# Moving the gate's weight rows by a few bytes in on-chip memory: banded attention with a gated linear unit on one Trainium2 core

## The chip, the cores and the metric

The kernel runs on one core of one Trainium2 chip. The core has a matrix engine (PE, whose weight loads are a stream of their own, PEld), a vector engine (DVE), a scalar engine (ACT), a general engine (POOL), a queue that issues transfers (SP) and 16 transfer engines (DMA). The metric is the device time of one launch in microseconds (us), as the median of several runs. Before the change three runs gave 852.70, 850.37 and 852.55 us, a median of 852.55 us.

## The reference, cut to what matters

Eight batches, eight heads, 512 local and 32 global positions, head size 64. Local positions attend to a band of 32 positions to each side and to the 32 global ones; global positions attend to all 544. What comes out, 8 x 544 = 4352 rows of 512 numbers, goes through a gated linear unit without a nonlinearity.

```python
s_ll = scale * np.matmul(q_l, k_l.transpose(0, 1, 3, 2))
mask = np.abs(pos[:, None] - pos[None, :]) <= window          # window = 32
s_ll = np.where(mask, s_ll, -1000000000.0)
s_l = np.concatenate([scale * np.matmul(q_l, k_g.transpose(0, 1, 3, 2)), s_ll], axis=-1)
out_l = np.matmul(sm(s_l), np.concatenate([v_g, v_l], axis=2))
...
x = np.ascontiguousarray(attn_out.transpose(0, 2, 1, 3)).reshape(B * S, H * D)
a = x @ w1
b = x @ w2
h = a * b @ w3
return (h @ w_out).astype(np.float32)
```

## The kernel before, in words

The 64 heads are worked off one after another: scores, softmax over the band, the product with v. Four pairs of heads make one batch's rows of x, turned so that the 512 features lie on 4 x 128 partitions and the tokens along the row. Behind each batch two passes of the gate run over 256 tokens each, woven between the next batch's attention steps; the rows of the global positions (8 x 32 = 256 tokens) make a seventeenth pass near the end. `w3` and `w_out` are multiplied with each other at the start (L917), so that a pass has only two layers: `first` (x with w1 and w2, L771 to L782) and `second` (the gated product with w3 times w_out, L810 to L812).

Numbers are split into a high and a low part, and each product is made from three matmuls on a 4-byte type: high with high, low of x with high of w, and high of x with low of w. These are the three lines L780, L781 and L782. In `first`, the row block `m` (0 to 7) of the output features and the half `c` (0 is w1, tile `ap`; 1 is w2, tile `bp`) choose a 128 x 128 piece of the weights for each of the four pairs `k`. So one call is twelve matmuls, and a pass has 16 calls. Over 17 passes this is 3264 matmuls, each with its own weight load. x is the operand that streams through PE (256 columns of 4 bytes, so 1024 bytes a partition); the weights are the operand that is loaded (128 columns, 512 bytes a partition). The weight load for the next matmul runs while the matmul ahead of it streams its x.

The weights lie in `W12[m]`, made by `alloc_w12` (L860): before the change a high and a low tile of `[128, 4, 2, 128]` words, 4096 bytes a partition each. They are filled once near the start of the span, blocks 0 to 3 in 512-word pieces and blocks 4 to 7 in 256-word pieces, by casts (L417, high part) and subtractions (L420, low part) on ACT, DVE and POOL, and stay for the whole launch. Blocks 4 to 7 take the place of the tiles of the opening (`wo`, `raw`, `w3f`), which are given up before.

By the addresses in the built program, all pieces of the weights start at a multiple of 256 bytes. The x tiles of the sixteen ordinary passes all start 192 bytes behind such a multiple, high and low part alike. Only the pass over the global positions differs, since its x borrows other tiles (`split_x`, L752): for pair 0 the high part starts at 128 and the low part at 0, for pair 1 at 192 and 64, for pairs 2 and 3 at 192 like all others. Below, the distance is the start of the weights less the start of x, modulo 256 bytes. Before the change it is 64 everywhere but in the pass over the global positions, where it is 128, 0 and 128 in the three matmuls of pair 0, and 64, 192 and 64 in those of pair 1.

What runs when is written out by hand: `ORDER_OF` gives every step its place in one list of all steps, and the engine for those that could run on several. Each engine works off its own steps in that order, with waits on the other engines where data or buffers ask for it.

Of the kernel before, what the change touches and what calls it, by code (L numbers as in the profile page):

```python
# [8 lines left out]
F32R = mybir.dt.float32r  # L9
# [21 lines left out]
START = (("s", 0), ("sg", 0), ("s", 1), ("sg", 1), ("s", 2), ("tg", 0))  # L31

# [9 lines left out]
def i(ap):  # L42
# [36 lines left out]
    load="9 6 49 79 389 416 974 1176 1480 1586 1810 1999 2236 2405 2762 2649 3179 1 3 58 14 16 142 56 75 160 140 203 "  # L79
# [4 lines left out]
    clear="0 22 7 4 2 10 530 524 536 517",  # L84
    warm="5 25",
    fetch="8 11 12 36 46 52 72 84 100 116 126 150 171 178 200 225 246 253 272 288 309 326 349 366 377 387 426 413 "
    "447 480 471 503 174 242 147 605 617 622 638 670 682 694 730 744 737 768 791 808",
    unit="24 23 31 35 37 43 45 42 48 64 65 68 77 76 81 94 86 96 112 109 114 119 118 122 141 133 144 149 148 165 173 "
# [7 lines left out]
    fold="53 71 90 131 157 195 207 213 66 87 97 102 162 202 218 226 264 269 291 308 321 324 329 332 258 276 296 315 "  # L96
    "347 353 356 364 360 370 374 381 395 402 410 417 407 421 424 436 442 448 457 463 452 485 523 527 548 560 583 588 "
    "493 497 515 538 554 566 572 579",
    w34h="A221 D237 D339 A378 A422 A468 A594 A585",
    w34l="254 250 350 386 431 472 598 589",  # L100
    qgh="A18 A19 P231 A322 P844 P925 P1291 D1294 A1704 A1772 P2121 P2136 P2569 P2638 D3000 P3049",
    qgl="P21 P20 P265 P331 D990 D949 D1298 D1299 D1790 P1842 P2189 D2166 D2576 P2644 D3104 D3074",
    vgh="D532 P565 A546 A561 P1093 P1149 D1141 A1101 A1549 A1573 P1552 D1559 P1964 P1984 A1995 D1990 P2383 A2407 "
    "A2411 D2420 P2811 P2872 D2855 A2847 P3241 A3253 D3269 P3289",
    vgl="D537 P587 P558 P590 D1152 P1156 P1143 P1121 D1555 D1584 D1579 P1561 P2036 P2031 D2003 P2007 P2429 D2424 "
    "P2441 D2438 D2835 P2897 D2908 P2865 P3265 D3271 D3283 D3292",
    Kh="D13 A47 D99 A177 P299 A439 A668 A809 A954 D1044 D1159 P1255 P1387 A1457 P1592 D1680 D1804 A1889 P2015 A2100 "
    "A2222 A2312 D2448 P2540 A2672 A2740 A2879 A2969 A3077 P3161 A3301 A3392",
    Kl="D15 P51 P107 P180 P307 P454 D684 D826 P963 D1050 P1167 P1259 P1390 P1460 P1610 P1683 D1806 P1893 D2025 P2104 "
    "P2227 P2323 P2460 D2549 P2678 P2746 P2886 D2976 D3089 P3165 D3315 P3396",  # L110
    sg="33 63 151 190 393 479 718 837 1005 1061 1220 1276 1416 1474 1646 1698 1850 1903 2055 2116 2269 2333 2496 "
    "2561 2703 2756 2931 2987 3135 3191 3348 3409",
    cg="D38 A67 D155 A193 A406 A483 A734 A841 A1023 A1068 D1230 A1280 A1434 A1481 A1650 A1705 A1855 A1910 D2071 "
    "A2120 A2275 A2338 A2501 A2564 A2718 A2766 A2935 A2991 A3138 A3194 A3353 A3413",
# [33 lines left out]
    exps="32 29 39 34 83 60 62 70 123 111 93 110 138 152 154 146 201 239 236 219 280 289 268 284 372 375 341 346 383 "  # L148
# [10 lines left out]
    t="41 117 145 185 248 311 427 482 533 628 703 793 863 931 991 1057",  # L159
# [143 lines left out]
def band_attention_glu_kernel(  # L303
# [72 lines left out]
    T = {}  # L376
# [483 lines left out]
    def alloc_w12(pool, m):  # L860
        W12[m] = tuple(P[pool].tile([128, 4, 2, 128], F32R, tag=f"w12{e}{m}", name=f"w12{e}{m}") for e in "hl")
# [582 lines left out]
```

## Time and profile before

One profiled execution took 853.9 us, its span on the core was 852.1 us, so 1.8 us lie around the span. The median of the runs is 1.35 us below this execution.

| engine | busy in the span | share | instructions |
|---|---|---|---|
| PE | 831.2 us | 98% | 5714 |
| PEld | 736.8 us | 86% | 5714 |
| DVE | 676.6 us | 79% | 1728 |
| ACT | 425.7 us | 50% | 1222 |
| POOL | 334.3 us | 39% | 499 |

The 3264 matmuls of L780 to L782 are well over half of PE's instructions. A matmul's row in the trace has a start and a length; lengths overlap, since the next matmul starts while the one ahead still drains. So the time that a matmul takes from its successors is read from start to start (a "step" below), not from the length. Start times in the timeline have two decimals of a microsecond, so a step is read over many matmuls: the start behind the last less the start of the first, by their count.

### The profile page before, as it was taken

Reading aid. Unit: us, or ns where it says so; the run is one execution under the profiler, and the core shown is the slowest. Engines: PE = TensorE matmul, PEld = TensorE weight load, DVE = VectorE, ACT = ScalarE, POOL = GpSimd, SP = SyncE. Lnnn points to the kernel's source line nnn. Section 1 sums busy time; section 2 is a strip of 40 time slices with the busy share of each in tenths; the row PEclk is TensorE's granted clock in tenths of the full one; section 3 lists DMA queues with packets and bytes.
Section 4 is the critical chain, followed back from the end, with each engine's and each line's share of the span. In section 5 each row is a group of like instructions: output and inputs, shape, how many; then the busy total and the mean of one; then the engine's idle time right before and its main releaser. Section 6 shows DMA issues by size and latency. Waiting matters only on the chain.

```text
span 852.1 us, 17311 instructions
## 1 busy us (share of the span) xinstructions
PE 831.2 (98%) x5714; PEld 736.8 (86%) x5714; DVE 676.6 (79%) x1728; ACT 425.7 (50%) x1222; POOL 334.3 (39%) x499
## 2 busy tenths in 40 slices
PE   7999999999999999999999999999999999999998
PEld 5554569898999889998999899999999999999997
DVE  5877899889897887888997978899888987854343
ACT  4765677755445565666556555664555455300000
POOL 2033465443443625354456555445345546200000
PEclk7999999999999999999999999999999999999999
DMA  7768845444566576667676665766676665410000
GB/s 244 235 212 250 232 112 157 131 121 100 143 171 167 141 186 169 177 171 180 151 201 162 164 163 149 202 168 172 171 174 175 166 158 149 116 33 25 1 25 26
DMA packets 101953, 128.85 MB, mean 151 GB/s; under 512 B 28648, under 2 KB 60904, under 8 KB 101864
## 3 DMA queue, kind: packets, MB, share of 16 engines
q1 hardware_dynamic: 101864, 127.75, 57.1%
q8 instruction: 45, 0.74, 0.4%
q14 instruction: 44, 0.36, 0.2%
HBM read 75.07 MB, written 25.30 MB: 118 GB/s over the span
## 4 chain that ended last, share of the span: by engine, by line
PE 78%; DVE 9%; DMA 6%; ACT 2%; issue 2%; SPq 2%; POOL 0%; DVEq 0%; ACTq 0%; POOLq 0%
PE w L917 7%; PE bp L780 6%; PE ap L780 6%; PE ap L781 6%; PE ap L782 6%; PE bp L781 6%; PE bp L782 6%; PE acc L810 6%; PE acc L812 6%; PE acc L811 6%; PE s L515 5%; PE av L644 5%; PE s L508 2%; PE av L636 2%; PE av L639 2%
## 5 line engine op out<-in xcount | busy, mean ns | idle before, releaser
L523 ACT ACTIVATE P<-P,mn 128x192 f32<-128x192 f32 (+1 forms) x256 | 121.4, 475 | 77.8 <-DVE mn L519 75.7
L780 PE MATMUL bp<-x,w12h 128*128 128x256 f32 x544 | 153.6, 282 | 0.9 <-DVE gl__2186 L420 0.5
L780 PE MATMUL ap<-x,w12h 128*128 128x256 f32 x544 | 153.1, 282 | 1.3 <-ACT as__6386 L417 1.3
L781 PE MATMUL bp<-x,w12h 128*128 128x256 f32 x544 | 151.7, 279 | 0.0
L782 PE MATMUL bp<-x,w12l 128*128 128x256 f32 x544 | 151.6, 279 | 0.0
L781 PE MATMUL ap<-x,w12h 128*128 128x256 f32 x544 | 151.5, 279 | 0.0
L782 PE MATMUL ap<-x,w12l 128*128 128x256 f32 x544 | 151.4, 278 | 0.0
L780 PEld LDWEIGHTS bp<-x,w12h 128*128 128x128 f32 x544 | 102.7, 189 | 3.1 <-DVE gl__2186 L420 0.7
L780 PEld LDWEIGHTS ap<-x,w12h 128*128 128x128 f32 x544 | 102.6, 189 | 2.9 <-ACT as__6386 L417 1.5
L781 PEld LDWEIGHTS bp<-x,w12h 128*128 128x128 f32 x544 | 102.6, 189 | 1.3 <-issue 0.2
L781 PEld LDWEIGHTS ap<-x,w12h 128*128 128x128 f32 x544 | 102.5, 188 | 1.3
L782 PEld LDWEIGHTS ap<-x,w12l 128*128 128x128 f32 x544 | 102.4, 188 | 0.0
L782 PEld LDWEIGHTS bp<-x,w12l 128*128 128x128 f32 x544 | 102.4, 188 | 0.0
L519 DVE CUSTOM_DVE_ANT_0 P<-s,cs 128x192 f32<-128x192 f32 (+1 forms) x256 | 88.0, 385 | 12.9 <-PE s L515 9.9
L917 PE MATMUL w<-wo,w3f 128*128 128x512 f32 x128 | 60.8, 613 | 0.0
L661 DVE TENSOR_TENSOR u<-av,cb 64x352 f32<-64x352 f32 x112 | 56.5, 517 | 4.0 <-ACT cb L417 2.4
L644 PE MATMUL av<-PTl__1012,vs 128*128 128x192 f32 x224 | 56.0, 276 | 0.0
L417 ACT COPY cb<-av 64x352 f32<-64x352 f32 x84 | 36.9, 448 | 37.5 <-PE av L644 33.1
L548 DVE STREAM_TRANSPOSE P<-P 128x640 f32<-128x640 f32 x48 | 40.4, 842 | 18.9 <-ACT P L523 18.6
L644 PE MATMUL av<-PTh__1022,vs 128*128 128x192 f32 x224 | 54.3, 267 | 0.8 <-ACT gh__3684 L417 0.4
L420 POOL TENSOR_TENSOR KE<-kr,KE 128x608 fp32r<-128x608 f32 x22 | 35.0, 1592 | 45.8 <-ACT KE L417 33.9
L420 POOL TENSOR_TENSOR qs<-qr,qs 64x512 fp32r<-64x512 f32 x31 | 40.6, 1310 | 27.6 <-ACT qs L417 15.3
(840 smaller groups left out, 2080.3 us busy)
## 6 DMA issues: line engine op xcount, KB each, us to landing
KO<-KE SPq DMA_DIRECT2D x56, 304.0 KB, 4.1
pd<-P SPq DMA_DIRECT2D x192, 80.0 KB, 2.3
raw_w<-in_w_t_dram SPq DMA_DIRECT2D x24, 512.0 KB, 4.8
RT<-pd SPq DMA_DIRECT2D x48, 256.0 KB, 3.0
kr<-in_kd_t_dram SPq DMA_DIRECT2D x32, 304.0 KB, 4.0
out_dram<-o SPq DMA_DIRECT2D x34, 256.0 KB, 3.0
KE<-KE SPq DMA_DIRECT2D x28, 304.0 KB, 3.4
qr<-in_q_t_dram SPq DMA_DIRECT2D x32, 256.0 KB, 3.6
```

The costliest lines, as they stand in the source:

```text
L420: (eng or nc.gpsimd).tensor_sub(dst, src, f(hi))
L519: nc.vector.tensor_tensor_reduce(blk(n, e), cut(n, T["st", n][:, e, 0 : WIN[e][1]]), cut(n, masks[e]), -0.125, 3.0e38, ALU.add, ALU.min, T ...
L523: nc.scalar.activation(blk(n, e), blk(n, e), AF.Exp, bias=T["mn", n][:, e : e + 1], scale=-1.0, accum_out=T["sm", n // 2][:, n % 2, e : e ...
L644: nc.tensor.matmul(av[:, o : o + c1 - c0], v, pt[:, j, c0:c1], start=False, stop=(j % 2 == y == 1), skip_group_check=True)
L661: nc.vector.tensor_add(T["u", n // 2][r : r + 64, x], T.pop(("av", n, x))[r : r + 64, 0:352], T["cb", n][r : r + 64, x])
L780: nc.tensor.matmul(d, wh[:, k, c, :], x[:, 0, 0:w], start=(k == m % 2 == 0), stop=False, skip_group_check=True)
L781: nc.tensor.matmul(d, wh[:, k, c, :], x[:, 1, 0:w], start=False, stop=False, skip_group_check=True)
L782: nc.tensor.matmul(d, wl[:, k, c, :], x[:, 0, 0:w], start=False, stop=(k == 3), skip_group_check=True)
L810: nc.tensor.matmul(a, gh[:, m % 2, sl], wh, start=(m == 0), stop=False)
L811: nc.tensor.matmul(a, gh[:, m % 2, sl], wl, start=False, stop=False)
L812: nc.tensor.matmul(a, gl[:, m % 2, sl], wh, start=False, stop=(m == 7))
L917: nc.tensor.matmul(T["w34", t], T["w3f", t, j // 4][:, j % 4], T["wo"][:, j], start=(j == 0), stop=(j == 7))
```

## The change

Each row block's high and low weights now lie in one tile of 2112 words (8448 bytes, 33 times 256), or 2048 words for block 7, and inside it they begin `SHIFT[m]` words from the tile's start. In bytes the shifts of the blocks 0 to 7 are 232, 240, 248, 8, 16, 24, 40 and 0. Modulo 256 the first three are the same as 24, 16 and 8 bytes less. Since every tile but the last is 33 times 256 bytes long, each still begins at a multiple of 256. The distance from the x of the ordinary passes becomes 40, 48, 56, 72, 80, 88 and 104 bytes for blocks 0 to 6, and stays 64 for block 7. No matmul, cast or transfer is added or taken away, and on each engine the instructions stand in the same order as before; the numbers of `ORDER_OF` differ by a few here and there, since they count places among steps of all engines.

```diff
+SHIFT = (58, 60, 62, 2, 4, 6, 10, 0)
...
     def alloc_w12(pool, m):
-        W12[m] = tuple(P[pool].tile([128, 4, 2, 128], F32R, tag=f"w12{e}{m}", name=f"w12{e}{m}") for e in "hl")
+        t = P[pool].tile([128, 2112 if m < 7 else 2048], F32R, tag=f"w12{m}", name=f"w12{m}")
+        t = t[:, SHIFT[m] : SHIFT[m] + 2048].rearrange("p (x k c w) -> p x k c w", x=2, k=4, c=2)
+        W12[m] = (t[:, 0], t[:, 1])
...
-    clear="0 22 7 4 2 10 530 524 536 517",
+    clear="0 22 7 3 2 10 528 522 534 516",
```

The last two lines stand for the whole table, whose rows all changed in this manner. By the built program, waits differ in a handful of places: the tiles of blocks 5 and 6, now further back, also touch one more of the buffers that the opening gave up, so POOL waits for one transfer more ahead of one cast of block 5 and of one of block 6.

More of the change, by code (lines that the diff above doesn't have):

```diff
@@ L96 @@
[L96 to L102, printed above, removed]
@@ L159 @@
-    t="41 117 145 185 248 311 427 482 533 628 703 793 863 931 991 1057",
-    hi="A50 D82 A54 A74 D69 P104 106 A130 D124 D132 A121 D127 A125 128 A161 A166 A175 A168 D163 A159 167 A197 D228 "
[12 rows of a table removed]
-    av="108 113 137 153 179 192 232 251 300 304 384 388 466 473 502 508 606 609 683 686 770 775 839 843 908 910 959 "
[5 rows of a table removed]
-    sum="D115 D129 D156 D169 D187 D205 A243 D277 D327 A343 D390 A394 D476 A501 D516 D542 613 621 692 697 781 785 852 "
[5 rows of a table removed]
-    inv="101 235 297 391 602 762 928 1031 1131 1229 1354 1445 1569 1658 1775 1861 1988 2066 2207 2282 2422 2525 2627 "
@@ new lines @@
+    "480 471 502 174 242 147 605 618 622 638 670 683 694 729 744 737 768 790 806",
+    unit="24 23 31 35 37 43 45 42 48 64 65 68 77 76 81 94 86 96 112 108 114 119 118 122 141 133 144 149 148 165 173 "
[7 rows of a table added]
+    fold="53 71 90 131 157 196 208 213 66 87 97 102 162 202 218 226 265 271 291 309 321 324 326 332 258 276 296 315 "
+    "347 352 356 364 359 371 374 381 395 401 412 417 408 420 423 436 442 448 457 463 452 485 523 527 545 559 582 586 "
+    "493 497 514 537 553 564 570 576",
+    w34h="A221 D237 D339 A378 A422 A468 A594 A584",
@@ new lines @@
+    w34l="253 249 350 386 431 472 597 588",
+    qgh="A18 A19 P231 A322 P844 P925 P1291 D1294 A1704 A1772 P2121 P2136 P2569 P2638 D3000 P3050",
+    qgl="P21 P20 P269 P330 D991 D949 D1298 D1299 D1790 P1842 P2189 D2166 D2576 P2644 D3104 D3075",
+    vgh="D532 P566 A547 A561 P1093 P1150 D1141 A1101 A1549 A1574 P1552 D1559 P1964 P1984 A1995 D1990 P2383 A2407 "
+    "A2411 D2421 P2811 P2874 D2856 A2847 P3241 A3254 D3269 P3290",
+    vgl="D539 P589 P558 P592 D1153 P1158 P1144 P1121 D1555 D1586 D1581 P1562 P2036 P2031 D2003 P2009 P2432 D2425 "
@@ new lines @@
+    "P2443 D2435 D2835 P2897 D2908 P2868 P3265 D3272 D3284 D3292",
+    Kh="D13 A47 D98 A177 P299 A439 A668 A809 A954 D1044 D1160 P1255 P1387 A1457 P1592 D1680 D1804 A1889 P2015 A2100 "
+    "A2222 A2313 D2448 P2541 A2673 A2740 A2880 A2969 A3076 P3161 A3300 A3392",
+    Kl="D15 P51 P107 P180 P306 P454 D684 D826 P963 D1050 P1168 P1259 P1390 P1460 P1610 P1683 D1806 P1893 D2025 P2104 "
+    "P2227 P2323 P2460 D2549 P2678 P2746 P2885 D2976 D3089 P3165 D3312 P3396",
+    sg="33 63 151 190 393 479 717 837 1005 1061 1219 1276 1416 1474 1646 1698 1850 1903 2055 2116 2269 2333 2496 "
@@ new lines @@
+    "2561 2703 2757 2931 2987 3135 3191 3348 3409",
+    cg="D38 A67 D155 A193 A405 A483 A735 A841 A1023 A1068 D1230 A1280 A1434 A1481 A1650 A1705 A1855 A1910 D2071 "
+    "A2120 A2275 A2338 A2501 A2565 A2718 A2766 A2935 A2991 A3138 A3194 A3353 A3413",
+    mg="40 73 158 198 414 492 741 848 1027 1074 1234 1285 1437 1484 1654 1712 1864 1919 2077 2126 2288 2341 2505 "
+    "2567 2732 2770 2937 2994 3153 3201 3368 3418",
+    eg="80 206 499 853 1079 1288 1490 1717 1924 2130 2348 2572 2775 2999 3207 3420",
@@ new lines @@
+    ng="85 216 504 857 1087 1295 1497 1722 1929 2141 2353 2581 2785 3003 3215 3425",
+    tg="95 222 519 860 1091 1302 1510 1725 1942 2151 2367 2585 2794 3009 3221 3439",
+    gw="A100 A103 D230 A234 A525 A530 D865 A869 A1097 A1103 A1313 A1315 A1518 A1520 A1732 A1735 A1949 A1951 A2159 "
+    "A2162 A2374 A2377 A2591 A2594 A2803 A2805 A3016 A3018 D3231 D3233 A3448 A3451",
+    ko="316 549 698 881 985 1117 1199 1323 1394 1530 1628 1749 1830 1960 2034 2172 2250 2387 2469 2605 2684 2816 "
+    "2896 3027 3109 3247 3335 3461",
@@ new lines @@
+    ke="403 580 746 911 1014 1137 1228 1343 1424 1565 1653 1780 1857 1987 2061 2195 2274 2415 2510 2636 2708 2845 "
+    "2940 3054 3139 3271 3362 3493",
+    vh="A521 A535 A715 A765 A856 D882 P972 D983 D1098 A1109 D1238 D1242 A1347 A1349 A1458 A1493 D1545 A1551 P1662 "
+    "A1664 P1761 D1777 P1876 A1880 A1979 D2057 A2111 A2149 A2201 A2204 P2297 P2304 D2412 A2420 P2519 D2526 A2626 "
+    "A2631 P2754 A2761 D2837 P2844 A2949 A2950 A3048 A3063 A3146 A3211 P3252 D3283 A3373 P3391 A3456 P3457 D3594 "
@@ new lines @@
+    "D3595",
+    vl="P543 P579 D759 P805 P862 P903 P1003 D984 D1188 D1148 D1243 D1247 D1364 P1399 D1489 P1501 P1548 D1558 P1668 "
+    "P1713 P1794 D1778 P1879 P1885 D2004 P2060 D2123 P2154 P2212 P2219 P2299 P2307 D2441 P2440 P2522 D2536 D2672 "
+    "P2635 D2760 P2783 D2853 D2870 P2960 P2965 P3056 D3069 P3186 P3218 P3291 P3287 D3387 P3424 D3501 P3491 P3606 "
+    "D3599",
+    s="17 44 78 120 170 241 282 337 430 541 640 690 785 876 948 980 1033 1111 1152 1190 1250 1319 1369 1388 1452 "
+    "1524 1584 1614 1671 1738 1797 1823 1884 1955 2008 2026 2089 2165 2218 2244 2295 2381 2442 2462 2534 2597 2657 "
@@ new lines @@
+    "2675 2735 2809 2869 2890 2964 3021 3070 3102 3155 3239 3293 3328 3386 3454 3511 3532",
+    mmax="26 27 28 30 55 57 58 61 88 89 91 92 134 136 139 142 181 182 183 184 256 257 261 268 293 298 300 317 355 "
[10 rows of a table added]
+    exps="32 29 39 34 83 60 62 70 123 111 93 110 138 152 154 145 201 239 236 219 281 289 267 284 372 375 341 346 383 "
[10 rows of a table added]
+    t="41 117 146 185 248 312 427 482 533 628 703 792 863 931 990 1057",
+    hi="A50 D82 A54 A74 D69 P104 106 A130 D124 D132 A121 D126 A127 129 A161 A166 A175 A168 D163 A159 167 A197 D228 "
[12 rows of a table added]
@@ new lines @@
+    av="109 113 137 153 179 191 232 252 301 304 384 388 466 473 500 508 606 609 682 686 770 775 839 843 908 910 959 "
[5 rows of a table added]
+    sum="D115 D128 D156 D169 D187 D204 A243 D277 D329 A343 D390 A394 D476 A503 D517 D542 613 621 692 697 781 786 852 "
[5 rows of a table added]
+    inv="101 235 297 391 602 762 928 1031 1131 1229 1354 1444 1571 1657 1775 1861 1988 2066 2207 2282 2423 2525 2627 "
+    "2724 2852 2932 3065 3147 3310 3389 3497 3573",
+    invo="105 238 310 406 607 773 930 1034 1146 1317 1365 1447 1587 1697 1801 1886 2018 2146 2277 2312 2430 2570 "
@@ new lines @@
+    "2630 2756 2858 2938 3095 3189 3343 3398 3500 3582",
+    invi="135 164 273 307 345 380 433 460 627 648 822 849 945 995 1048 1078 1194 1241 1337 1360 1419 1451 1487 1509 "
+    "1608 1687 1741 1758 1851 1883 1918 1936 2094 2140 2185 2209 2291 2309 2344 2364 2513 2540 2600 2616 2700 2733 "
+    "2778 2791 2889 2966 3004 3034 3149 3168 3206 3226 3379 3406 3455 3471 3518 3554 3611 3619",
+    join="P186 D283 P399 P548 P700 P866 P1007 P1102 P1267 P1372 D1476 D1531 P1694 P1785 P1902 P1962 P2127 P2217 "
@@ new lines @@
+    "P2332 D2388 P2538 D2647 P2765 D2817 P2963 D3064 P3182 P3249 D3415 D3498 D3588 D3638",
+    joing="189 287 415 568 748 874 1026 1155 1271 1393 1576 1622 1703 1846 1935 2038 2170 2241 2414 2468 2557 2694 "
+    "2911 2968 3040 3083 3199 3321 3419 3509 3590 3642",
+    mul="P199 D194 P340 P323 D428 P421 P552 P616 P742 P713 P870 P895 P1017 P1020 P1106 P1128 P1289 P1278 P1406 P1412 "
[3 rows of a table added]
+    xh="D211 A205 P351 P334 P432 P469 A560 D629 A905 A864 P907 P906 A1021 A1108 D1110 D1145 A1316 A1303 A1422 A1421 "
[3 rows of a table added]
@@ new lines @@
+    xl="P224 P209 P354 P335 D484 P490 D562 P693 D914 P909 D933 D935 D1030 D1186 D1112 P1181 P1320 P1309 P1427 D1443 "
[3 rows of a table added]
+    gout="229 313 419 575 755 891 1105 1207 1275 1544 1603 1685 1745 1911 2001 2054 2214 2356 2433 2516 2655 2860 "
+    "2947 2979 3047 3172 3243 3382 3428 3514 3596 3645",
+    qh="A286 A449 A567 A650 A740 P845 A880 P955 P987 P1076 P1116 P1164 A1214 A1284 D1324 A1376 A1403 A1511 A1570 "
+    "A1590 A1619 A1708 P1748 A1803 A1829 A1899 P1986 A2014 P2042 P2096 D2174 P2224 D2251 A2302 D2410 A2447 P2486 "
@@ L213 @@
+    "A2554 P2622 A2661 A2683 A2789 A2815 A2875 A2912 A2988 A3025 P3078 P3108 A3183 A3246 P3307 A3333 P3407 A3459 "
     "P3517",
[L214 to L216 removed]
+    ql="D302 D501 D604 P653 P778 D859 D929 P958 P994 P1081 D1133 D1177 P1222 D1312 D1326 P1380 P1433 D1519 D1582 "
@@ L243 @@
-    "2219 2281 2318 2371 2437 2500 2531 2587 2659 2715 2742 2798 2867 2927 2957 3013 3076 3126 3157 3231 3298 3352 "
-    "3385 3444 3504 3561 3587",
-    gin="3475 3530 3608 3663",
-    first="599 612 592 620 632 648 655 663 707 732 752 760 828 855 818 847 867 879 923 941 901 934 965 973 951 1009 "
[9 rows of a table removed]
+    lo="578 595 593 565 569 D587 P598 636 679 657 660 673 P637 P641 751 749 747 730 734 P754 D766 804 835 833 810 "
[10 rows of a table added]
+    cb="D610 A617 A687 A691 A779 A782 A846 A850 D912 A919 D964 D969 A1041 A1045 A1090 A1092 D1204 A1210 A1227 D1240 "
[6 rows of a table added]
@@ new lines @@
+    T="1058 1136 1180 1218 1277 1345 1391 1430 1480 1550 1612 1640 1700 1763 1828 1856 1912 1981 2035 2059 2115 2190 "
+    "2243 2273 2328 2413 2464 2484 2556 2634 2682 2712 2764 2840 2894 2913 2989 3055 3093 3133 3185 3274 3322 3361 "
+    "3410 3477 3533 3568",
+    dw="1066 1140 1187 1231 1283 1351 1400 1438 1491 1556 1616 1656 1707 1771 1838 1871 1922 1989 2039 2084 2122 "
+    "2199 2255 2296 2347 2419 2478 2489 2560 2640 2690 2725 2782 2850 2904 2918 2993 3061 3098 3140 3195 3278 3326 "
@@ L256 @@
+    "3365 3416 3483 3539 3571",
+    dr="1086 1154 1217 1249 1307 1368 1428 1461 1514 1578 1644 1673 1729 1783 1863 1892 1945 2007 2074 2105 2156 "
+    "2220 2281 2318 2371 2437 2500 2531 2587 2659 2715 2742 2798 2865 2927 2957 3013 3079 3126 3157 3229 3299 3352 "
+    "3385 3444 3503 3561 3587",
+    gin="3474 3530 3608 3664",
+    first="599 612 591 619 632 647 656 665 707 733 752 760 828 855 819 847 867 879 923 941 901 934 965 973 951 1009 "
[9 rows of a table added]
     "3643 3648 3649 3652 3653 3656 3659 3666 3667 3670 3672 3674 3678 3681 3682 3686 3691 3694 3699 3703 3705 3708 "
@@ L266 @@
+    gb="630 688 777 871 950 981 1035 1107 1149 1200 1252 1314 1357 1396 1442 1500 1575 1621 1682 1715 1781 1839 1872 "
+    "1934 2005 2053 2112 2182 2231 2287 2321 2373 2431 2479 2512 2584 2643 2693 2727 2780 2862 2920 2961 3035 3097 "
+    "3132 3173 3227 3286 3341 3370 3430 3489 3512 3585 3612 3654 3668 3676 3690 3706 3716 3727 3736 3751 3759 3771 "
     "3779",
-    gh="A635 A705 A783 A877 A957 A1008 A1060 D1113 A1166 A1222 D1263 D1317 A1372 A1410 A1446 A1512 A1580 A1625 D1691 "
[2 rows of a table removed]
+    gh="A635 A705 A784 A877 A957 A1008 A1060 D1113 A1165 A1221 D1263 D1318 A1371 A1409 A1446 A1513 A1580 A1625 D1691 "
[2 rows of a table added]
@@ L274 @@
+    "1900 1952 2012 2083 2138 2200 2252 2294 2339 2380 2439 2492 2533 2601 2658 2701 2752 2807 2867 2929 2997 3071 "
+    "3107 3144 3198 3238 3294 3354 3394 3445 3496 3544 3592 3628 3657 3671 3680 3693 3709 3719 3730 3739 3754 3763 "
     "3774 3782",
-    second="675 696 722 743 796 807 888 913 982 998 1022 1052 1070 1104 1147 1157 1186 1212 1244 1253 1279 1286 1334 "
[5 rows of a table removed]
+    second="675 696 722 743 796 808 888 913 982 997 1022 1052 1070 1104 1147 1156 1185 1211 1245 1253 1279 1286 1334 "
[5 rows of a table added]
     "3781 3783 3784 3785 3787",
-    out="A927 D956 A1179 A1168 A1378 A1373 D1560 A1564 A1791 A1796 D1992 A1996 A2247 A2272 A2418 A2427 A2653 A2664 "
@@ L283 @@
-    "A2843 A2840 A3110 A3105 D3264 A3318 A3489 A3495 D3658 D3644 D3700 D3701 D3745 D3746 D3786 D3789",
-    store="932 1329 1264 1172 1540 1701 1694 1820 1973 2117 2137 2397 2402 2545 2621 2773 2671 2975 2984 3193 3257 "
-    "3376 3286 3602 3528 3604 3660 3662 3702 3704 3747 3749 3788 3790",
+    out="A927 D956 A1178 A1167 A1379 A1373 D1561 A1563 A1791 A1796 D1993 A1996 A2247 A2272 A2418 A2426 A2653 A2665 "
+    "A2843 A2839 A3110 A3105 D3264 A3315 A3488 A3495 D3658 D3644 D3700 D3701 D3745 D3746 D3786 D3789",
@@ L286 @@
+    store="932 1328 1264 1172 1539 1701 1693 1821 1972 2117 2137 2395 2400 2545 2621 2774 2670 2975 2984 3192 3256 "
+    "3376 3285 3601 3527 3604 3660 3662 3702 3704 3747 3749 3788 3790",
 )
```

81 lines of the change are left out of this document (6 added, 75 removed), and 186 rows, old and new, of tables (av, cb, exps, first).

## Prediction

> **What bounds the kernel now.** I read the page first (engines, slices, chain), then PE's waits, the groups by line, and last the timeline of PE. The page's engine row, its clock row and the head of its chain:
>
> ```profile
> PE 831.2 (98%) x5714; PEld 736.8 (86%) x5714; DVE 676.6 (79%) x1728; ACT 425.7 (50%) x1222; POOL 334.3 (39%) x499
> ...
> PEclk7999999999999999999999999999999999999999
> ...
> PE 78%; DVE 9%; DMA 6%; ACT 2%; issue 2%; SPq 2%; POOL 0%; DVEq 0%; ACTq 0%; POOLq 0%
> ```
>
> PE is in work nearly everywhere, at its full granted clock behind the first slice, and 78% of the chain that ends last lies on it. The two longest waits of PE on others, and two stages (one of the attention's, one of the last passes; the numbers behind the comma are the busy time of PE, PEld, DVE, ACT and POOL, each with its instructions):
>
> ```profile
> PE sg L693 <- DVE mn L519: 5.1, 3, 4.0
> PE av L639 <- DVE G__1037 L420: 3.8, 4, 1.5
> ```
>
> ```profile
> 500.00:600.00 100.00, 98.66 (x743) 93.47 (x742) 85.74 (x219) 55.73 (x161) 49.95 (x75) 1.00 0.66 170
> ...
> 750.00:780.00 30.00, 30.00 (x223) 28.44 (x222) 12.24 (x20) 0.00 (x0) 0.00 (x0) 1.00 0.07 23
> ```
>
> So a microsecond that PE loses is lost to the launch. One that PE gains is not quite gained, since DVE is 86% busy in the middle and 9% of the chain is on it: I pass on 0.8 of a gain (PE's 78% and the 2% of issue), all of a loss in the stretches that only PE sets, and 0.9 of a loss over the whole span.
>
> The change touches only the weights of `first`. Its second and third line, from the groups (busy us, mean ns of one, idle before):
>
> ```profile
> L781 PE MATMUL bp<-x,w12h 128*128 128x256 f32 x544 | 151.7, 279 | 0.0
> L782 PE MATMUL bp<-x,w12l 128*128 128x256 f32 x544 | 151.6, 279 | 0.0
> L781 PE MATMUL ap<-x,w12h 128*128 128x256 f32 x544 | 151.5, 279 | 0.0
> L782 PE MATMUL ap<-x,w12l 128*128 128x256 f32 x544 | 151.4, 278 | 0.0
> ```
>
> The mean of 279 hides two values. Here are two undisturbed stretches of the last passes, L781 alone (length of one, min/median/max), the first from 748.3 to 758.2 us, the second from 836.0 to 843.2 us:
>
> ```profile
> L781 PE MATMUL ap<-x,w12h x16: 281/281/281, 748.4 to 756.6; 128*128 128x256 f32 x16
> ...
> L781 PE MATMUL bp<-x,w12h x12: 281/281/281, 751.3 to 758.0; 128*128 128x256 f32 x12
> ```
>
> ```profile
> L781 PE MATMUL bp<-x,w12h x13: 276/276/276, 835.8 to 842.6; 128*128 128x256 f32 x13
> ...
> L781 PE MATMUL ap<-x,w12h x8: 276/276/276, 837.5 to 839.9; 128*128 128x256 f32 x8
> ```
>
> Each stretch has one length throughout. The steps from start to start differ with them; the first row and the row behind the last of each stretch:
>
> ```profile
> 748.31 0.28 PE L780 MATMUL ap<-x,w12h 128*128 128x256 f32 x1
> ...
> 758.20 0.40 PE L810 MATMUL acc<-w34h,gh__10084 128*128 128x512 f32 x1
> ```
>
> ```profile
> 835.73 0.28 PE L780 MATMUL bp<-x,w12h 128*128 128x256 f32 x1
> ...
> 842.87 0.39 PE L810 MATMUL acc<-w34h,gh__10805 128*128 128x512 f32 x1
> ```
>
> The first stretch holds 84 matmuls of `first` (28 of L781, three lines): 9.89 us / 84 = 117.7 ns a step, **the long step**. The second holds 63 (21 of L781): 7.14 / 63 = 113.3 ns, **the short step**. Same operands, same clock, nothing else running that PE waits for: a stream of such matmuls can settle into either and stays there. Which share has which follows from the four means: (278.75 - 276) / (281 - 276) = 0.55 of the matmuls have the long length. I take half, so a step is 115.5 ns on average, and half of 3264 steps could become 4.4 ns shorter or longer.
>
> **The change part by part.** *Casts, subtractions and transfers.* Their number, size and engine stay. The shifts are whole multiples of 8 bytes. The two added waits stand on POOL ahead of casts of blocks 5 and 6; the buffers they ask after were last used by the opening:
>
> ```profile
> L417 POOL CAST w12h<-raw_w12s x6: 412/419/534, 123.6 to 145.0; 128x256 fp32r<-128x256 f32 x6
> ...
> L420 DVE TENSOR_TENSOR w12l<-raw_w,w12h x4: 676/680/821, 101.2 to 122.0; 128x512 fp32r<-128x512 f32 x4
> ```
>
> The last reading of the opening's raw weights starts at 122.0 us, so their transfers landed before, and the first of these casts starts at 123.6. Cost 0. Without that cover POOL's queue behind the cast would be late by a part of one cast (0.4 us) once; too little to count.
>
> *Tile size.* Every tile is 33 x 256 bytes, so the shifts arrive at the matmuls as written, and x does not move. That the change doesn't reach PE is excluded.
>
> *The distance itself.* 7/8 of 3264 = 2856 matmuls get a new distance, 24 bytes less to 40 more than the 64 of today. No row shows such a distance, so I bound its price from the rows that differ in it: the pass over the global positions, where pair 0 has 128, 0 and 128, pair 1 has 64, 192 and 64, and pairs 2 and 3 have 64. Two calls of `first` in a row, each twelve steps in order of the pairs; the rows at which a pair's steps begin:
>
> ```profile
> 787.60 0.28 PE L780 MATMUL ap<-x,w12h 128*128 128x256 f32 x1
> ...
> 787.96 0.29 PE L780 MATMUL ap<-x,w12h 128*128 128x256 f32 x1
> ...
> 788.32 0.28 PE L780 MATMUL ap<-x,w12h 128*128 128x256 f32 x1
> ...
> 789.00 0.28 PE L780 MATMUL ap<-x,w12h 128*128 128x256 f32 x1
> ...
> 789.36 0.29 PE L780 MATMUL ap<-x,w12h 128*128 128x256 f32 x1
> ...
> 789.72 0.28 PE L780 MATMUL ap<-x,w12h 128*128 128x256 f32 x1
> ...
> 790.40 0.28 PE L780 MATMUL bp<-x,w12h 128*128 128x256 f32 x1
> ```
>
> Pair 0 takes 0.36 us for three steps (120 ns), pair 1 another 0.36 (120), pairs 2 and 3 together 0.68 for six (113.3); the next call repeats it: 0.36, 0.36, 0.68. Only x's place differs between the pairs. So the distance counts, and 64, the one that the change leaves, is the only one in the trace at which the short step is seen.
>
> Upper end: all 2856 at pair 0's 120 ns instead of 115.5 is 2856 x 4.5 = 12.9 us lost. Lower end, from the nearest row of a matmul that is not slowed: four fp32 transposes of 128 columns, and their length:
>
> ```profile
> 258.39 0.60 PE L730 MATMUL tg<-cs,Pg 128*128 128x128 f32 x4
> ```
>
> ```profile
> L730 PE MATMUL tg<-cs,Pg 128*128 128x128 f32 x64 | 9.7, 273 | 0.9 <-DVE Pg L724 0.9
> ```
>
> (0.60 - 0.273) / 3 = 109 ns a step. If every shifted matmul came to that, 2856 x 6.5 = 18.6 us, 0.8 of it 14.9 us gained.
>
> Between them I take a straight line from 115.5 ns at 64 bytes to 120 ns at 64 bytes to either side (0 and 128): 0.07 ns a byte. The seven shifts are 24, 16, 8, 8, 16, 24 and 40 bytes off, 19.4 on average: 1.36 ns x 2856 = 3.9 us, 0.9 of it 3.5 us. This sits nearer to no change than to the upper end, since the shifts are small beside 64 bytes. In terms of the two steps it says that about a third of all shifted matmuls, so well over half of those with the short step, lose it (1.36 / 4.4 = 0.31).
>
> **Sum.** 853.9 + 3.5 = 857.4 us on the profiled execution's terms (its span of 852.1 and 1.8 around it). The median of the runs is 852.55, so 1.35 below that execution: 856.0 us.
>
> **The rivals.** *The distance only matters when it is large, or not at all.* For it: at one distance, 64, both steps occur in long stretches (the rows at 748 and 835 us), so something else picks the step, and it may be the moment at which the stream starts. Against it: pairs 0 and 1 above. Time: 852.5 us. The Trainium skill, SBUF — State Buffer, section "Who interferes with whom", gives PE two read ports that are independent of each other, one for the streamed operand and one for weight loads, so that by that rule no distance would count and the time would stay at 852.5 us; the rows of pairs 0 and 1 disagree with it, by some 7 ns a step.
>
> *The shifts throw the stream out of the long step.* This ends on the faster side. A stream in the long step stays in it while all distances are alike (84 steps from 748.31 us). Now the distance changes at each border between row blocks, every 12 to 24 steps. If such a jolt brings the stream to the short step and the new distances keep it there, half of 2856 steps become 4.4 ns shorter: 6.3 us, 0.8 of it 5.0 us gained: 847.5 us. For it: in the pass over the global positions a stream that changes its distance all the time comes back to 113.3 within pairs 2 and 3. Against it: the same jolts cost 120 ns in pairs 0 and 1 first. It decides if, behind a border, fewer than about half of the jolts go the wrong way.
>
> *The shifts free the matmul of its delay*, down to the transposes' 109 ns: 852.5 - 14.9 = 837.6 us. Nothing in the trace shows a 256-column matmul of this type at that step.
>
> *The short step is lost at all shifted blocks*: 2856 / 2 x 4.4 = 6.3 us, or 12.9 at pair 0's step: 858.8 to 865.4 us. This is the forecast's upper half and no case of its own.
>
> **How the numbers follow.** Forecast (some of the short steps lost) 0.45, its own range 853 to 864 us; no effect 0.24; thrown out of the long step 0.27; free of delay 0.04. A measurement of this kernel tells about 0.3% from no change, so 850.0 to 855.1 us counts as the same. The forecast's lowest part falls into that (0.07 of its 0.45); of the case without effect 0.19 is the same and the rest is split to both sides; of the two faster cases 0.03 is the same. Slower 0.38 + 0.02 = 0.40, same 0.07 + 0.19 + 0.03 = 0.29, faster 0.28 + 0.03 = 0.31. The range reaches from below the case of 847.5 to the upper end of the price: 845 to 864 us; it leaves out the 109 ns case and the corners of the others.
>
> **What would show it.** In the changed profile the lengths of L780 to L782 in the last passes, block by block: if 276 ns is rare on shifted blocks and 281 or more is common, while the last block keeps both, the forecast holds. If the share of 276 is as before on all blocks, the case without effect does. If stretches start at 281 and end at 276 at a border of blocks, the jolt does. The steps on the blocks 6 (40 bytes off) should be worse than on 2 and 3 (8 off); if the order is another, the straight line was wrong even where the sum is right. A DVE wait of PE that grows would show that more of a gain is held back than 0.2 of it.

## The result, and the profile after

The changed kernel takes 858.02 us (median of 4 runs, 857.60 to 858.49); the kernel before took 851.71 beside it (median of 4, 850.37 to 852.70). The ratio is 1.0074, with a 95% interval of 1.0055 to 1.0093: 6.3 us slower. The forecast was 856.0, on the slower side, with a range of 845 to 864.

The engine row and the head of the chain, from the page of the changed kernel:

```profile
PE 839.6 (98%) x5714; PEld 745.4 (87%) x5714; DVE 673.9 (79%) x1728; ACT 425.4 (50%) x1222; POOL 332.0 (39%) x499
...
PE 78%; DVE 7%; DMA 7%; ACT 3%; issue 2%; SPq 1%; POOL 1%; DVEq 0%; ACTq 0%; POOLq 0%
```

PE is busy 8.4 us longer with the same 5714 matmuls; DVE, ACT and POOL are each within 3 us of before. The groups of the second and third line of `first`, now L784 and L785 (busy us, mean ns of one, idle before):

```profile
L784 PE MATMUL ap<-x,w 128*128 128x256 f32 x544 | 152.8, 281 | 0.4 <-DVE x L423 0.4
L785 PE MATMUL bp<-x,w 128*128 128x256 f32 x544 | 152.7, 281 | 0.0
L784 PE MATMUL bp<-x,w 128*128 128x256 f32 x544 | 152.6, 281 | 0.0
L785 PE MATMUL ap<-x,w 128*128 128x256 f32 x544 | 152.6, 281 | 0.0
```

The mean length of one went from 278 or 279 ns to 281. It is again a mean of several lengths, so the steps have to be read from the start times. A stretch of the last passes shows it block by block. In the timeline of PE, by the program's order, block 6 (distance 104) begins at 773.49 us, block 7 (distance 64, not shifted) at 774.94 and block 6 again at 776.32; the second layer follows at 777.75:

```profile
773.49 0.28 PE L783 MATMUL ap<-x,w 128*128 128x256 f32 x1
...
774.94 0.28 PE L783 MATMUL ap<-x,w 128*128 128x256 f32 x1
...
775.29 0.28 PE L783 MATMUL ap<-x,w 128*128 128x256 f32 x1
...
776.20 0.28 PE L785 MATMUL ap<-x,w 128*128 128x256 f32 x1
776.32 0.28 PE L783 MATMUL bp<-x,w 128*128 128x256 f32 x1
...
777.75 0.40 PE L813 MATMUL acc<-w34h,gh__10222 128*128 128x512 f32 x1
```

Block 6 takes 1.45 us for twelve steps (121 ns each), then block 7 from its fourth matmul on 0.91 us for eight (114 ns), then block 6 again 1.43 us for twelve (119 ns). Three steps behind the border into block 7 this stream has the short step. Not every one gets there: of the 14 streams that cross from block 6 into block 7 in the ordinary passes, 4 are at the short step in the second half of the call (its seventh to eleventh step, 113.2 to 113.6 ns on average), and before the change 9 of 14 were, in the all-zero kernel below 10 of 14. So block 7 may pay for its neighbour, though its own distance is the old one; 14 streams of one execution are too few to be sure.

For the comparisons below, every step of `first` inside a stream of the ordinary passes was read from the start times in the trace and put under its distance: the start of the weights that are being loaded less the start of the x that streams, modulo 256. "Mean" is that of the steps under 135 ns (longer ones hold a wait), "short" the share of at most 114 ns. Before: 115.64 ns with 51% short. The changed kernel:

| block | 0 | 1 | 2 | 7 | 3 | 4 | 5 | 6 |
|---|---|---|---|---|---|---|---|---|
| distance, bytes | 40 | 48 | 56 | 64 | 72 | 80 | 88 | 104 |
| mean, ns | 118.97 | 118.17 | 118.15 | 116.51 | 118.35 | 118.82 | 115.32 | 119.36 |
| short | 0% | 1% | 8% | 33% | 1% | 1% | 59% | 6% |

The three lines of `first` together, start to start, took 389.8 us before and 395.7 after: 5.9 us more. Waits that fall into these lines are counted there; without them it is 382.8 and 389.8 us, 7.0 more. The rest of PE's lines took 1.5 us longer. The span of the two profiled executions grew by only 3.7 us, because the one before holds longer waits of PE (those on DVE were 5.1 and 3.8 us at the largest two). After, they are:

```profile
PE av L642 <- DVE G__1031 L423: 2.7, 3, 1.2
PE sg L696 <- DVE mn L522: 2.2, 4, 1.0
```

All waits of PE sum to 16.7 us before and 12.0 after. The all-zero kernel below, which has the old distances, has 13.0; so the new distances do not explain the difference. With one execution each more can't be said, and the medians' 6.3 us are the better figure.

### The profile page after: what moved, and what is told of

Same layout as the page of the kernel before. It is cut to its first block, busy times and chain, and to the rows that moved or that the text cites. A ratio compares the mean times of both kernels' runs of the same rounds, so it can differ in the third digit from the quotient of the medians.

```text
span 855.8 us, 17312 instructions
## 1 busy us (share of the span) xinstructions
PE 839.6 (98%) x5714; PEld 745.4 (87%) x5714; DVE 673.9 (79%) x1728; ACT 425.4 (50%) x1222; POOL 332.0 (39%) x499
## 4 chain that ended last, share of the span: by engine, by line
PE 78%; DVE 7%; DMA 7%; ACT 3%; issue 2%; SPq 1%; POOL 1%; DVEq 0%; ACTq 0%; POOLq 0%
PE bp L783 7%; PE ap L783 6%; PE bp L785 6%; PE bp L784 6%; PE ap L784 6%; PE ap L785 6%; PE acc L813 6%; PE acc L815 6%; PE acc L814 6%; PE s L518 5%; PE av L647 5%; PE w L922 4%; PE av L642 2%; PE sg L696 2%; DMA raw_w<-in_w_t_dram 1%
## 5 line engine op out<-in xcount | busy, mean ns | idle before, releaser
L783 PE MATMUL ap<-x,w 128*128 128x256 f32 x544 | 154.3, 284 | 0.9 <-ACT as__6377 L420 0.9
L783 PE MATMUL bp<-x,w 128*128 128x256 f32 x544 | 154.5, 284 | 0.5 <-DVE gl__2178 L423 0.5
L784 PE MATMUL ap<-x,w 128*128 128x256 f32 x544 | 152.8, 281 | 0.4 <-DVE x L423 0.4
L785 PE MATMUL bp<-x,w 128*128 128x256 f32 x544 | 152.7, 281 | 0.0
L784 PE MATMUL bp<-x,w 128*128 128x256 f32 x544 | 152.6, 281 | 0.0
L785 PE MATMUL ap<-x,w 128*128 128x256 f32 x544 | 152.6, 281 | 0.0
L783 PEld LDWEIGHTS ap<-x,w 128*128 128x128 f32 x544 | 102.6, 189 | 2.5 <-ACT as__6377 L420 1.1
L783 PEld LDWEIGHTS bp<-x,w 128*128 128x128 f32 x544 | 102.7, 189 | 2.4 <-DVE gl__2178 L423 0.7
L784 PEld LDWEIGHTS ap<-x,w 128*128 128x128 f32 x544 | 102.7, 189 | 2.0 <-DVE x L423 0.6
L784 PEld LDWEIGHTS bp<-x,w 128*128 128x128 f32 x544 | 102.6, 189 | 1.3 <-issue 0.2
L785 PEld LDWEIGHTS ap<-x,w 128*128 128x128 f32 x544 | 102.6, 189 | 0.0
L785 PEld LDWEIGHTS bp<-x,w 128*128 128x128 f32 x544 | 102.5, 188 | 0.0
```

Source lines behind the costliest of these rows:

```text
L783: nc.tensor.matmul(d, wh[:, k, c, :], x[:, 0, 0:w], start=(k == m % 2 == 0), stop=False, skip_group_check=True)
L784: nc.tensor.matmul(d, wh[:, k, c, :], x[:, 1, 0:w], start=False, stop=False, skip_group_check=True)
L785: nc.tensor.matmul(d, wl[:, k, c, :], x[:, 0, 0:w], start=False, stop=(k == 3), skip_group_check=True)
```

## The experiments

Three theories were set against each other and against the prediction's straight line. **A**: each distance has its own steady steps. **B**: the jolt at a border between blocks of different distance costs. **C**: the new tiles, the moved tiles of the opening or the added waits cost, and no distance does. All kernels are the changed one with other shifts, unless the edit says more; where block 7 is shifted, its tile is wider by the shift. The medians of the kernel before, taken beside them, lay between 850.3 and 851.1 us. Where only a `+SHIFT` is shown, it stands in place of the change's line.

**All shifts zero.** New tiles, old distance 64 everywhere.

```diff
-SHIFT = (58, 60, 62, 2, 4, 6, 10, 0)
+SHIFT = (0, 0, 0, 0, 0, 0, 0, 0)
```

> All shifts 0, in the new tiles (high and low part in one tile, 256 spare bytes): every distance is 64 again. Theory A (each distance has its own steady step): as before, 852 us within 2, steps of the ordinary passes a mix of 113 and 118 ns, mean 115.7. Theory B (what costs is the jolt when the distance changes from block to block): the same 852. Theory C (the new tiles, the moved opening tiles or the added waits cost the time): 858.

Measured: 850.28 us, ratio 0.9988 (0.9975 to 1.0000). Steps of 115.35 ns, 56% short. C falls: the tiles and the waits cost nothing that can be seen.

**All blocks at distance 88.** No borders between distances.

```diff
+SHIFT = (6, 6, 6, 6, 6, 6, 6, 6)
```

> All eight blocks shifted by 24 bytes: the distance is 88 everywhere, with no border at which it changes. Theory A, by block 5 of the changed kernel (88 bytes, mean step 115.3 ns although it enters from blocks with other distances, most steps at 113): nearly all steps at 113 to 114 ns, 3264 x 2.1 ns = 6.9 us less, 0.8 of it gained: 846 us. Theory B: no border, so as before, 852. The straight line of the prediction (0.07 ns a byte off 64): 1.7 ns more a step, 857.

Measured: 851.14 us, ratio 1.0003 (0.9991 to 1.0016); 115.19 ns, 64% short. The gain I looked for did not come: a uniform stream at 88 has a long step of its own (328 of 2857 steps at 120 ns), as 64 has its 118.

**All blocks at distance 104.**

```diff
+SHIFT = (10, 10, 10, 10, 10, 10, 10, 10)
```

> All eight blocks shifted by 40 bytes: the distance is 104 everywhere. Theory A, by block 6 of the changed kernel (119.4 ns): 3264 x 3.7 ns = 12 us, 0.9 of it: 862.5 us, hardly a step at 113. Theory B: no border, 852. The straight line: 2.8 ns a step, 860.

Measured: 860.25 us, ratio 1.0105 (1.0079 to 1.0132); 119.27 ns, 9% short. One line of the groups of this kernel:

```profile
L784 PE MATMUL ap<-x,w 128*128 128x256 f32 x544 | 153.8, 283 | 0.4 <-DVE x L423 0.4
```

The mean length is 283 without a single border, and the step is that of block 6 in the changed kernel (119.36). The time alone does not tell A (862.5) from the straight line (860), but the step does: the line gives 115.64 + 2.8 = 118.4 ns. So the distance decides, and B is not needed for the loss.

**Three surveys**, each with eight distances in one kernel: multiples of 32 or 16; multiples of 8; and odd numbers of words.

```diff
+SHIFT = (8, 12, 16, 24, 32, 40, 48, 56)      # first, distances 96 112 128 160 192 224 0 32
+SHIFT = (38, 34, 54, 52, 50, 14, 26, 22)     # second, 216 200 24 16 8 120 168 152
+SHIFT = (63, 61, 1, 3, 5, 7, 11, 13)         # third, 60 52 68 76 84 92 108 116
```

> Blocks 0 to 7 shifted by 32, 48, 64, 96, 128, 160, 192 and 224 bytes: distances 96, 112, 128, 160, 192, 224, 0 and 32, read from the step of each block. The straight line: 117.7 ns at 96 and 32, 118.9 at 112, 120 at 128 and 0 and beyond. Theory A with a pattern that repeats every 128 bytes: 192 is like 64 (a mix of 113 and 118), 224 like 96, 160 like 32, 128 like 0 (about 120). With a pattern that repeats every 64 bytes: 128, 192 and 0 are all like 64, and 96, 160, 224 and 32 all alike.

> Blocks 0 to 7 at the distances 216, 200, 24, 16, 8, 120, 168 and 152, read from the step of each block. Theory A with a pattern that repeats every 128 bytes: 216 is like 88 (mean about 115.3, more than half of the steps at 113), 200 like 72 (118.4), 168 like 40 (119.0), 24 and 152 alike, 8 and 120 not far from 0 (119.2). With no such repetition: 216 is like its neighbours 200 and 224, 117 to 119. The straight line with its low point at 64 alone: all eight at 120 or above but 24 (118.3).

> Shifts by odd numbers of words: distances 60, 52, 68, 76, 84, 92, 108 and 116 for blocks 0 to 7. If the step depends on 8-byte pairs, each is like one of its neighbours (84 or 92 like 88 with half its steps at 113, 60 or 68 like 64). If single words count, all eight are off 64 and 88 and hardly a step is at 113: 118 to 119.5 throughout. The straight line of the prediction: 115.8 at 60 and 68, 116.3 at 52 and 76, up to 119 at 116.

Measured: 857.64, 855.54 and 856.47 us in one execution each. Mean step in ns, with the share of short steps where it is over 5%:

| distance | mean | distance | mean | distance | mean |
|---|---|---|---|---|---|
| 0 | 119.24 | 76 | 114.86, 72% | 128 | 118.99 |
| 8 | 116.62 | 84 | 119.89 | 152 | 117.66, 10% |
| 16 | 118.23 | 92 | 118.43 | 160 | 119.45 |
| 24 | 118.94 | 96 | 118.20 | 168 | 117.81, 31% |
| 32 | 118.29 | 108 | 120.65 | 192 | 116.82, 25% |
| 52 | 116.44, 44% | 112 | 119.52, 9% | 200 | 117.75 |
| 60 | 119.61 | 116 | 118.75 | 216 | 118.97, 5% |
| 68 | 118.48 | 120 | 118.70 | 224 | 117.24, 10% |

There is no line in this. With the table above, the short step is common at 52, 64, 76 and 88, which lie 12 bytes apart, and nearly absent at 56, 60, 68, 72, 80 and 84 between them. At 192 and 168 it comes in part. In the timeline of the third survey, block 2 (68) begins at 825.63 us and block 3 (76) at 827.05; the second layer follows:

```profile
825.63 0.28 PE L783 MATMUL bp<-x,w 128*128 128x256 f32 x1
...
827.05 0.28 PE L783 MATMUL bp<-x,w 128*128 128x256 f32 x1
...
828.41 0.39 PE L813 MATMUL acc<-w34h,gh__10657 128*128 128x512 f32 x1
```

Twelve steps take 1.42 us at 68 (118.3 ns) and 1.36 us at 76 (113.3 ns).

**x moved instead of the weights.** A wider tile ahead of x moves x (and the gated product) by 32 bytes; the weights of blocks 0 to 6 stay at multiples of 256, block 7's lie 32 behind one.

```diff
-            T["mg", m // 2] = p1.tile([128, 1], F32, tag="mg", name=f"mg{m}")
+            T["mg", m // 2] = p1.tile([128, 9], F32, tag="mg", name=f"mg{m}")[:, 0:1]
+SHIFT = (56, 56, 56, 56, 56, 56, 56, 0)
```

> All x of the ordinary passes moved up by 32 bytes (one small tile ahead of them is longer), the weights of blocks 0 to 6 moved back to a multiple of 256 as before the change, block 7 at 32 bytes behind one. So blocks 0 to 6 have their old place and a new distance, 32; block 7 has a new place and the old distance, 64. Theory A (the distance counts): blocks 0 to 6 at 118.3 as block 7 of the first survey, with no step at 113; block 7 has steps at 113. If the weights' own place counts: blocks 0 to 6 as before the change, 115.6 with half the steps at 113, and block 7 worse.

Measured: 858.54 us in one execution; 118.31 ns on blocks 0 to 6 (distance 32), 114.99 with 66% short on block 7 (distance 64). The first survey had 118.29 at distance 32 with the weights moved. So at these two distances it is the distance between the operands that counts, and not the place of either.

**64 and 88 in turn.**

```diff
+SHIFT = (0, 6, 0, 6, 0, 6, 0, 6)
```

> Blocks 0, 2, 4, 6 at distance 64, blocks 1, 3, 5, 7 at 88, the two that have the short step. If a border between blocks throws a stream out of the long step (the prediction's second rival): the stretches that stay long at one distance end at the next border, share of 113 up from 0.56 to 0.64 to 0.75 or more, 847 us. If each distance keeps its own long step (118 and 120) across the border: as the two kernels with one distance, 850 to 851 us. If a border costs steps of its own: 853 or more.

Measured: 850.37 us, ratio 1.0005 (0.9992 to 1.0017). 115.40 ns with 57% short at 64, 114.93 with 64% at 88: the values of the two uniform kernels. Six changes of distance a pass inside its streams cost nothing, and here they win nothing: B, as a price of every border, falls.

**All blocks at 72, the smallest shift of the change.**

```diff
+SHIFT = (2, 2, 2, 2, 2, 2, 2, 2)
```

> All eight blocks shifted by 8 bytes, distance 72: the smallest shift of the change alone. In the changed kernel the block at 72 had 118.35 ns a step with neighbours at 56 and 80. Theory A: 3072 x (118.35 - 115.64) = 8.3 us, 0.9 of it 7.5 us, so 858 us where before takes 850.5. Straight line: 8 bytes cost 0.56 ns, 3072 x 0.56 x 0.9 = 1.5 us, so 852. If it is not the distance of 72 but its changing neighbours that cost, about 851.

Measured: 857.04 us, ratio 1.0070 (1.0045 to 1.0095); 118.33 ns, no short step. Eight bytes on every block cost nearly as much as the whole change; the straight line had given them 1.5 us.

**All blocks at 76.**

```diff
+SHIFT = (3, 3, 3, 3, 3, 3, 3, 3)
```

> All eight blocks shifted by 12 bytes, so a distance of 76 for every matmul of the ordinary passes. In the survey with odd words the block at 76 had 114.86 ns a step and 72% of its steps at 113 or 114, the highest share of all distances seen, though its neighbour blocks lay at 68 and 84. Theory A (each distance has its own steady steps): 3072 x (115.64 - 114.86) = 2.4 us less than before, with 0.8 of it passed on 848.5 us where before takes 850.5; if the share rises to 0.9 without hostile neighbours (113.8 ns), 3072 x 1.84 = 5.7 us, so 846. Straight line of the prediction: 12 bytes off 64 cost 0.84 ns, 3072 x 0.84 x 0.9 = 2.3 us, so 853. If a uniform stream locks into a long step of its own at 76, as it did at 88 (120), same as before within 0.3%.

Measured: 849.49 us, ratio 0.9981 (0.9965 to 0.9998); 114.67 ns, 76% short. L785 in the last passes, from 742 to 774 us, first of the kernel at 76 and then of the one at 72 (length of one, min/median/max):

```profile
L785 PE MATMUL ap<-x,w x32: 276/276/281, 744.9 to 769.2; 128*128 128x256 f32 x32
```

```profile
L785 PE MATMUL ap<-x,w x29: 277/280/283, 749.7 to 773.7; 128*128 128x256 f32 x29
```

Four bytes between them, and 276 is the median in the first row and does not occur in the second.

**76 and 88 in turn.**

```diff
+SHIFT = (3, 6, 3, 6, 3, 6, 3, 6)
```

> Blocks in turn at 76 and 88 bytes, the two distances besides 64 at which the short step was common. The alternation of 64 and 88 gave 115.25 ns a step and 850.37 us where before took 850.34. Theory A with the shares of the single blocks (114.9 and 115.0): 3072 x 0.7 = 2.1 us less, 0.8 passed on: 848.7. If changing distances keep a stream out of any long step (the rival that ended on the faster side): 113.6 ns, 3072 x 2.0 x 0.8 = 4.9 us less, 845.5. If the borders cost: 851 or more.

Measured: 848.63 us, ratio 0.9972 (0.9956 to 0.9989), the fastest of all runs: 0.28% under the kernel before, just within what the prediction counted as no change, with an interval that ends below 1. The same two calls of `first` in the kernel at 76 and in this one, behind the scores of the global positions (L696):

```profile
504.63 0.70 PE L696 MATMUL sg<-KE,QG 128*128 128x288 f32 x4
505.16 0.28 PE L783 MATMUL bp<-x,w 128*128 128x256 f32 x1
...
506.60 0.28 PE L783 MATMUL bp<-x,w 128*128 128x256 f32 x1
...
508.04 0.29 PE L642 MATMUL av<-G__1031,vgs__993 128*128 128x288 f32 x1
```

```profile
503.84 0.70 PE L696 MATMUL sg<-KE,QG 128*128 128x288 f32 x4
504.37 0.28 PE L783 MATMUL bp<-x,w 128*128 128x256 f32 x1
...
505.81 0.28 PE L783 MATMUL bp<-x,w 128*128 128x256 f32 x1
...
507.17 0.29 PE L642 MATMUL av<-G__1031,vgs__993 128*128 128x288 f32 x1
```

With 76 in both blocks each call takes 1.44 us (120 ns a step): the stream starts in the long step and stays in it over the border. With 76 and 88 the first call takes 1.44 us and the second 1.36 (113.3): the border threw the stream out of the long step. That is the rival which ended on the faster side, seen at work.

It is no single case. Take every stream that is at 119 ns or more in the second half of a call and goes on into the next call. In the uniform kernels all 15 (6 at 76, 9 at 88) are still there a call later; at a border between 76 and 88, all 6 of this kernel and all 4 of the next one have reached the short step. From 64's own long step of 118 ns it is otherwise: in the kernel with 64 and 88 in turn, 19 streams came to a border into 88 in it, and 4 reached the short step behind it. So a border helps some pairs of distances and not others. The gain is small, too: the interval overlaps that of the uniform kernel at 76 (0.9965 to 0.9998).

**The second layer moved too.** As the kernel before it, with `w34` moved by 116 bytes, so that the second layer's distance (gated product, which is loaded, less `w34`, which streams) becomes 76 where it was 192. To make room, the weights of blocks 0 to 3 share one tile. Instructions and waits keep their order.

```diff
-            W34[t] = tuple(const.tile([128, 512], F32R, tag=f"w34{e}{t}", name=f"w34{e}{t}") for e in "hl")
+            if t in (0, 7):
+                T["u"] = const.tile([128, 64 + (6144 if t == 0 else 2048)], F32R, tag=f"w34{t}", name=f"w34{t}_"), 29
+            u, o = T["u"]
+            T["u"] = u, o + 1024
+            W34[t] = (u[:, o : o + 512], u[:, o + 512 : o + 1024])
```

> As the alternation of 76 and 88, and the streamed operand of the second layer (w3 times w_out, 512 columns) moved by 116 bytes too, so that the loaded gated product, which stays at its place, lies 76 bytes from it where it was 192. Instructions and waits stay in the same order. In the alternation of 76 and 88 a step of these lines took 231 ns on average with 226 ns the commonest at the first of the three (twice the short step of 256 columns is 226.6); with the distance at 224 in the kernel that moved x it took 232 to 236 ns. Theory A, if the same distances serve streams of 512 columns: 816 x 4.0 = 3.3 us less, 0.8 of it passed on, so 2.6 us under the 848.6 of the alternation: 846. If 512 columns have other good distances: between 848 and 851. The straight line (12 bytes off 64 against 128 bytes off) gives about the same as theory A, so this run does not tell these two apart.

Measured: 852.71 us, ratio 1.0021 (1.0008 to 1.0035), so 4.1 us above the kernel it was to improve. `first` kept its time (385.6 us against 385.5); the three lines of the second layer went from 191.4 to 198.3 us. A stretch of them near the end (the shared tile of `w34` is `w__495` there), first at distance 192 (23 steps between the two rows), then at 76 (9 steps):

```profile
836.84 0.39 PE L813 MATMUL acc<-w34h,gh__10797 128*128 128x512 f32 x1
...
842.11 0.40 PE L815 MATMUL acc<-w34h,gl__10855 128*128 128x512 f32 x1
```

```profile
842.80 0.40 PE L813 MATMUL acc<-w__495,gh__10780 128*128 128x512 f32 x1
...
844.95 0.40 PE L813 MATMUL acc<-w__495,gh__10780 128*128 128x512 f32 x1
```

5.27 us / 23 = 229 ns a step, against 2.15 / 9 = 239. The distance counts in the second layer as well, but it has other good distances: 76, the best of the table for `first`, is the worse one here. Whether that comes from its 512 columns or from something else in which the two layers differ, no run shows. My expectation carried the table over, and missed.

What the shifts did to `first`, and what the launch kept of it, against the all-zero kernel (span 849.3 us, `first` 388.8):

| kernel | `first`, us | change | span, us | change |
|---|---|---|---|---|
| the change | 395.7 | +6.9 | 855.8 | +6.5 |
| all at 104 | 397.7 | +8.9 | 858.1 | +8.8 |
| all at 72 | 394.0 | +5.2 | 854.4 | +5.1 |
| all at 88 | 387.3 | -1.5 | 849.1 | -0.2 |
| all at 76 | 386.3 | -2.5 | 847.7 | -1.6 |
| 64 and 88 in turn | 387.6 | -1.2 | 848.1 | -1.2 |
| 76 and 88 in turn | 385.5 | -3.3 | 846.1 | -3.2 |

## Why the prediction was right, and where it was not

**The side and its reason held.** The forecast case was that shifted blocks lose their short steps. Six of seven did, nearly wholly (0 to 8% short, from 51%), and the time rose by 6.3 us where 3.5 were forecast.

**The term that was mis-sized** is the price of the distance, 1.36 ns x 2856 = 3.9 us. Measured, `first` took 5.9 us more than before and 6.9 us more than in the all-zero kernel, which is 2.07 to 2.42 ns for each shifted matmul. The step that failed is the straight line from 64 bytes outwards, 0.07 ns a byte. It put 8 bytes at 0.56 ns; the uniform kernel at 72 shows 118.33 - 115.64 = 2.7. It put 24 bytes at 1.7 ns; block 5, at 88, got 0.3 ns shorter. The prediction said that another order of the blocks would show the line wrong even if the sum were right, and that is how it came: block 6 (40 off) is 1 ns worse than blocks 2 and 3 (8 off), where the line has 2.2, and block 5 (24 off) is the best of all. Some of the error cancelled, since one of seven blocks kept its pace while the other six paid 2.5 to 3.7 ns, more than the 2.2 that half the matmuls make by losing the short step. The upper half of the forecast, "the short step is lost at all shifted blocks", 858.8 at its lower end, describes six of the seven. That the total came within about 2 us is therefore in part luck of the seven distances: for 76 and 88 on all blocks the same line gave 853 and 857 us, and they took 849.49 and 851.14, where the kernel before took 851.12 and 850.88.

**What passes on.** 0.9 of a loss was taken; the table shows 0.94 to 0.99. 0.8 of a gain was taken; single executions show from 0.1 to 1.0, too spread to test it. The sign that I had named for a gain held back, a growing wait on DVE, tells nothing: the wait of the global scores on DVE was 4.8 and 5.1 us in the two kernels that gained least of it (76 and 88), and 5.1 in the one that lost most (104).

**Nothing for the rest.** The added waits, the tiles and the casts were put at nothing; the all-zero kernel at 0.9988 confirms it.

**The rivals.** That no distance counts falls by the uniform kernels at 72 and 104. The Trainium skill, SBUF — State Buffer, section "Who interferes with whom", has PE's port for the streamed operand and its port for weight loads independent of each other; by that the uniform kernels would all take the same time, and they take 849.49 (76) to 860.25 us (104) with instructions alike in number, size and order. Where the two operands lie in relation to each other matters here; whether that is a matter of ports the runs cannot say. That borders throw the stream out of the long step was a real mechanism with a condition that failed: the new distance must have a short step to go to. At 76 and 88 in turn it has, and all ten streams that came to such a border at 120 ns left it there; at 64 and 88 in turn it has, and most did not, so the condition alone is not enough. At six of the seven distances of the change the short step hardly occurs. At the seventh, 88, 15 of the 16 streams that came from block 4 were at the short step by the second half of block 5, where before the change 8 of 16 were; the uniform kernel at 88 has 14 of 16 at the same place, so this is the distance and not the border. That the matmul is freed down to 109 ns was not seen in any kernel.

## What to carry to other kernels

Where a matrix engine is fed by back-to-back matmuls that each load new weights, read the step from start to start, not the mean length, and look whether it takes several values at one shape: the relative byte address of the two operands may be worth some per cent of it (114.67 to 119.27 ns in the uniform kernels here). Such a price has no slope to be read from two far points; vary the distance in steps of one word, and for each layer anew, since the table for `first`, with 256 columns, did not serve the second layer, with 512. A survey with one distance a block gives eight points from one run, and a uniform kernel then tests the best.

## What the runs showed that was not expected

At uniform distances the mean step of a 256-column matmul ran from 114.67 ns (76) to 119.27 (104), and 4 bytes (76 to 72) moved it by 3.7 ns. The good distances 52, 64, 76 and 88 lie 12 bytes apart, but 40, the next one down, has no short step, and 100 was not tried; why is open. The repetition after 128 bytes is only partial: 0 and 128 agree (119.24 and 118.99), while 192 has half the short steps of 64 (25 against 51%), and 224 is 1 ns below 96.

At two distances where the short step is rare or absent, the steps repeat a pattern. At 104, in the changed kernel, steps of 118, 118, 120 and 124 ns came round again and again from 776.3 us; at 32, in the kernel that moved x, the twelve steps of a call (122, 118, 116, 122, 116, 116, 120, 116, 123, 117, 117, 122) came back value by value at 752.9, 755.8 and 758.6 us.

At 64, 76 and 88 the same operands can run in a short or a long step (113.3 against 118, 120 and 120 ns) for as long as the stream lasts. At 88 there is a third pace of 116 to 117 ns, and of 11 streams that ended a call in it in the uniform kernel, 4 were at the short step a call later. What picks one at the start is only partly seen: the quoted stream at 76 that starts behind the scores of the global positions goes into the long step, while those at 76 behind the second layer in the last ordinary passes of that kernel reach the short one after three steps in seven of eight cases, and after seven in the other. What sets it was not settled.
